# One fused attention and gated MLP kernel, its 1134 operations put in another order

## The chip, the cores and the metric

The kernel runs on one core of a Trainium2 chip. Its engines work side by side, each on its own instructions in the order given: TensorE (PE in the profile, with its weight loads as PEld), VectorE (DVE), ScalarE (ACT), GpSimd (POOL), and SyncE (SP), whose queue issues the transfers. They hand over through semaphores. The metric is the device time of one execution in microseconds. Before the change the median of three runs is 200.47 us (199.44 to 200.6).

## The reference

Two stages. The first is causal attention on 4 batches of 8 heads, 768 positions, 64 channels, in which each query sees only the six chunks of 32 keys with the highest bound:

```python
k_min, k_max = min and max of each chunk of 32 keys
ub = sum_d maximum(q * k_min, q * k_max)          # one bound per query and chunk
ub = where(causal, ub, -1e9); top_chunks = the 6 largest per query
scores = q @ k.T / 8, kept where the chunk is in top_chunks and causal
attn = softmax(scores); x = attn @ v              # heads side by side: 4 x 768 x 512
```

The second is a gated MLP with a spatial product over the 768 positions:

```python
h = maximum(x @ w_in, 0); u, v = halves of h      # 512 columns each
v_n = (v - mean(v)) / sqrt(var(v) + 1e-6)
v_s = w_spatial @ v_n + b_spatial
out = (u * v_s) @ w_out
```

## The kernel before, in words

Two heads make a pair: pairs 0 to 15, four to a batch. The first four pairs are worked in halves of 384 positions, a and b. After each batch's four pairs comes its MLP, six tiles of 128 rows; MLP work of one batch stands between attention work of the next.

The code builds a list of named operations with their inputs, outputs and buffer pools (`load` L502, `prep` L523, `attend` L716, `mlp` L865). A string, `ORDER` (L160), then says in which order they are issued, on which engine and in which buffers. A word such as `c_k0aA:0` is operation c_k0a on ScalarE with place 0 of its pool; P is TensorE, D VectorE, A ScalarE, G GpSimd, S the SP queue. `replay` (L115) takes the words one by one and checks that inputs come first and buffers are free, and the operations are emitted in that order (L997 and on). No scheduler moves anything afterwards. Each engine keeps its own words in the string's order, so an operation that waits holds back all later words of its engine.

The operations of a pair, by name: ld_k, ld_q, ld_v load; c_k, c_q, c_v cast to fp16 (the helper `copy`, L310, whose lines are L312 on ScalarE and L314 on VectorE and GpSimd); t_ transposes on TensorE (L561) and e_ brings the result out of PSUM; from pair 10 on x_kq transposes by DMA instead (L569), c_s spreads the queries for the wide form and kw copies the keys for it. kmm are the chunk maxima and minima (L593, VectorE), km their copy into place, rq the relus of q (L607 to L611), ub the bound's product (L628), max its eight largest (L650, L655), grd a guard column (L665, L667), sel the selection mask (L678 to L683), tsel and es its transpose (L701), sc the scores (L745 and L758, L780 in the wide form), exp the exponentials (L794, ScalarE), tri the causal cut of the diagonal (L805, GpSimd), av the product with v (L828), rec and nrm the division (L834, L839), tx, ex and xx the transposes of x (L860, L849).

Of the MLP: v and u are the two projections (L877) with relus rv and ru (L884 ScalarE, L886 VectorE); bn, ag, ln, rs the statistics (L895 to L904), vn the normalisation (L909, VectorE); s the spatial product (L925), g the gate (L929), xg or tg and eg the transpose of the gated tile (L950, L938), o the last product (L961), eo its copy out of PSUM, so the store (L968). c_wv, c_wu, c_wo and ld_ws, c_ws, tws, ews prepare the weights. The operations w0 to w3 (L453) are products of zeros, nine, three, five and two of them, that keep TensorE going at the start. presets (L434 to L437, L986) clear buffers; preset_kw copies `expand` into the wide key buffers.

PSUM holds two pairs of banks for scores and four general buffers (`gen`); SBUF has eight places for raw loads (`st`), nine half-size ones (`hst`), seven for exponentials and so on:

```python
RINGS = {"hst": 9, "st": 8, "kqT": 6, "kq16": 2, "x16": 2, "x16d": 2, "e": 7, "vraw": 6, "fold": 1, "sn": 3, "selT": 5, "qs": 2}
WARM = (9, 3, 5, 2)
```

The relus of q may run on GpSimd in the halves of the first pairs; the old order puts none there:

```python
op(f"rq{m}_{tag}", {"DVE": 465.0 if half is None else 265.0, "ACT": t_act(ns) + 40.0,
                    **({} if half is None else {"POOL": 1450.0})}, go, ...)
```

The numbers beside the engines are costs for whoever searches an order; nothing in the program reads them when it is replayed.

Of the kernel before, what the change touches and what calls it, by code (L numbers as in the profile page):

```python
# [163 lines left out]
ub0aP:2 max0aD:0 c_k3aG:3 grd0aG:0 t_q1aP:3 c_k1aA:0 expandA:0 t_k1aP:0 sel0aD: c_k2aG:1 e_k1aA:1 c_k0bG:2 t_k3aP:1  # L164
tsel0aP:2 t_k2aP:0 es0aD:0 e_q1aA: rq1_1aA:1 kmm1_1aD:1 preset_km0G: kmm0_1aD: km0_1aG:3 km1_1aG: ld_q2aS:8 c_q2aG:0
e_k2aA:2 e_k3aA:3 c_q3aA:3 preset_sn1G: kmm0_2aD:2 kmm1_2aD: sc0a_0P:10 t_k0bP:3 ub1aP:2 t_q2aP:0 t_q3aP:1 ld_q1bS:0
ld_q0bS:1 kmm0_3aD:0 c_q1bG:1 c_q0bD:2 ld_k1bS:2 ld_k3bS:3 ld_wu1S:0 ld_k2bS:4 ld_q2bS:5 ld_q3bS:7 ld_k4S:1 ld_v1aS:6
max1aD:1 preset_vt5G: grd1aG:0 c_k1bG:0 preset_km4D: exp0a_01A:0 km0_2aG:0 exp0a_00A: e_q2aA: km1_2aA: e_k0bA:
c_k3bG:3 sel1aD: ld_v0aS:8 ld_ws1S:2 ld_q4S:3 ld_v3aS:0 ld_q7S:4 ld_wv0S:5 ld_v2aS:1 ld_wv3S:6 ld_k5S:7 e_q3aD:
rq1_2aD:0 rq1_3aD:1 kmm1_0bD:1 kmm0_0bD: w0P:0 tsel1aP:0 t_q1bP:2 t_q0bP:3 t_k3bP:1 es1aA:1 ub2aP:0 sc1a_0P:10  # L170
km1_0bG: e_q1bA: e_q0bA: preset_snb1D: max2aD:0 kmm1_3aD: sel2aD:0 c_k2bG:1 c_q2bG:2 km0_0bA: rq1_0bA:0 grd2aA:
km0_3aG:4 km1_3aG: ub0bP:2 tsel2aP:3 max0bD:1 es2aD:2 sel0bD:1 e_k3bA: exp1a_00A:1 exp1a_01A: c_q3bG:3 ub3aP:0
t_q2bP:1 t_k1bP:3 e_k1bA: e_q2bA: c_wu1G:0 rq1_1bD:0 max3aD:0 sel3aD:0 preset_vt2D: c_v0aA:1 c_k4G:2 c_v1aG:3
preset_snb0D: t_k2bP:2 sc2a_0P:10 exp2a_00A:2 exp2a_01A: e_k2bD: grd3aG: grd0bG: av1aP:3 tsel3aP:1 tsel0bP:0
kmm1_1bD:2 es3aD:3 kmm1_2bD:1 rec1aD:0 kmm1_3bD:0 kmm0_1bD: av0aP:2 t_k4P:1 rec0aD:1 kmm0_3bD: nrm1aD:0 nrm0aD:1
kmm0_2bD: rq1_2bA:1 es0bA:4 c_q4G:0 e_k4A:4 km0_1bG: c_ws1G:1 c_v3aG:5 km1_1bG: sc3a_0P:10 exp3a_00A:3 exp3a_01A:
t_q3bP:0 t_q4P:1 e_q4A: e_q3bD: tws1P:3 ub1bP:2 max1bD:0 ews1D:0 sel1bD:0 c_q7G:2 sc0b_0P:10 c_v2aG:2 c_wv0G:0 tx0aP:0
av2aP:1 km0_2bA: km1_2bG: av3aP:3 ex0aD:0 rec2aD:2 nrm2aD:1 grd1bA: tsel1bP:2 ub2bP:0 max2bD:1 rec3aD:0 exp0b_01A:4
exp0b_00A: tx2aP:1 sc0b_1P:01 nrm3aD:1 tx3aP:3 c_k5G:3 c_wv3G: preset_sna1G: tri0b_00G: km1_3bG: ld_wu2S:0 c_wu2G:
km0_3bG: grd2bA:1 es1bA:0 rq1_3bA:0 ld_wv1S:1 ld_wv2S:3 ld_q6S:2 ld_wu3S:4 ld_k6S:5 c_wv2G: c_wv1G: sel2bD:  # L180
exp0b_11A:5 exp0b_10A: ex2aD: ex3aD: kmm1_4D:2 t_q7P:2 rq1_4D:1 e_q7D:5 kmm0_4D: t_k5P:0 km0_4G:2 tx1aP:1 ex1aA:
e_k5A:0 tsel2bP:3 sc1b_0P:10 ub3bP:1 max3bD:0 sel3bD:0 v0_1P:0 rv0_1D:0 c_k6D:0 es2bD:1 km1_4G: grd3bG: c_wu3G:
tri0b_10G: exp1b_01A:6 exp1b_00A: v0_2P:2 sc1b_1P:01 tsel3bP:1 rv0_2A:1 ld_v0bS:2 ld_wu0S:7 c_wu0D: c_q6D:1 es3bD:2
c_v0bG: ld_v1bS:3 ld_q5S:6 ld_k8S:0 ld_q9S:3 exp1b_10A:1 exp1b_11A: t_k6P:0 av0bP:2 e_k6A:1 bn0_1D:0 bn0_2D:1
tri1b_10G: c_q5G:2 tri1b_00G: c_q9G:3 ld_ws2S:1 c_ws2G:0 ld_ws5S:4 ld_k7S:5 ld_v4S:7 ld_v2bS:4 ld_ws0S:2 ld_v3bS:5
ld_k9S:6 t_q6P:3 ub4P:1 e_q6A: sc2b_0P:01 max4D:1 rec0bD:1 nrm0bD:1 ag0_1D:0 t_q5P:0 u0_1P:3 u0_2P:2 exp2b_01A:0
exp2b_00A: tri2b_00G: c_k8D:1 c_v1bD: rq1_6D:0 preset_km1D: sel4D:1 e_q5D: kmm0_5D:1 kmm1_5D: ru0_1A:0 ru0_2A:1 grd4A:
# [28 lines left out]
tri9_10G: grd11G: c_s12G:0 tri9_00G: rv1_2A:3 km0_12A: v1_4P:3 o0_5P:0 ag1_1D:2 rq0_12D: ub12P:2 bn1_2D:1 exp9_20A:2
exp9_21A: eo0_5A:2 eo0_4A:1 rv1_4D:4 bn1_5D:2 sc10_0P:10 exp10_01A:6 exp10_00A: v1_3P:0 av8_0P:3 av8_1P:1 sc10_1P:01
ld_q15S:7 xs11S:3 ld_k14S:4 so0_4S: ld_v11S:1 x_kq13S:4 max12D:0 ag1_5D:3 sel12D: ag1_2D: bn1_0D:0 rec8_0D:2 bn1_4D:2
rec8_1D:1 rv1_3A:0 ld_v10S:3 ld_v12S:5 ld_q14S:6 tri9_20G: av9_1P:2 u1_3P:0 nrm8_1D:0 bn1_3D:1 ag1_0D: exp10_11A:1
# [813 lines left out]
```

## Time and profile before

| | us |
|---|---|
| median of three runs | 200.47 |
| the profiled execution | 198.78 |
| its span, first to last instruction | 197.1 |
| TensorE busy | 186.9 |
| VectorE busy | 163.0 |
| ScalarE busy | 144.5 |
| GpSimd busy | 89.9 |
| granted TensorE clock | 1.000 |

The durations below come from the profiled execution, whose own time is 1.7 us under the median. Groups of the profile read: line, engine, operation, output<-input, shapes, count | busy us, mean ns of one | idle time of the engine before them and what ended it. Stretches of time are given from the start of the span. Matmuls overlap their neighbours, so that a busy TensorE may have small holes, and a matmul's mean duration is longer than the distance to the next one.

### The profile page before, as it was taken

The page shows a single profiled execution, that of the slowest core. Times are in us where ns is not written, and L with a number is a line of the kernel's source. Part 1 is how long each engine was busy: PE and PEld are TensorE (multiplying, and loading weights), DVE is VectorE, ACT ScalarE, POOL GpSimd, SP SyncE. Part 2 cuts the span into 40 slices and gives each one's busy share as a digit, 9 for nine tenths or more (in the row PEclk, how much of TensorE's full clock was granted, in tenths as well). Part 3 has the DMA queues.
Part 4 walks back from the last instruction along what each step waited for, and adds up shares of the span by engine and source line. Part 5 has one row for each costly group of instructions (what it writes and reads, how often), then busy time and mean ns, then how long its engine had stood idle before and what let it go on. Part 6 is the DMA issues. An engine that isn't in the chain of part 4 may idle for free.

```text
span 197.1 us, 5797 instructions
## 1 busy us (share of the span) xinstructions
PE 186.9 (95%) x2201; PEld 107.7 (55%) x2201; DVE 163.0 (83%) x499; ACT 144.5 (73%) x233; POOL 89.9 (46%) x175
## 2 busy tenths in 40 slices
PE   7799989999999899999999999999999999999992
PEld 2356665566656255664367566545675664444450
DVE  2798999999899999997999999996995644894521
ACT  3889999889999976896898895598877541464051
POOL 3479696758578886553343191245540410000000
PEclk9999999999999999999999999999999999999999
DMA  5999999999998969699999999895930357501654
GB/s 161 315 325 350 331 321 330 336 255 327 235 251 199 245 137 168 145 188 192 286 221 283 243 172 149 189 241 174 253 69 0 92 121 216 161 37 71 161 213 160
DMA packets 98139, 41.01 MB, mean 208 GB/s; under 512 B 85440, under 2 KB 92864, under 8 KB 98112
## 3 DMA queue, kind: packets, MB, share of 16 engines
q1 hardware_dynamic: 97968, 40.38, 81.9%
q8 instruction: 17, 0.28, 0.6%
q10 hardware_dynamic: 144, 0.26, 0.3%
q14 instruction: 10, 0.08, 0.1%
HBM read 24.38 MB, written 6.29 MB: 156 GB/s over the span
## 4 chain that ended last, share of the span: by engine, by line
PE 70%; DVE 20%; issue 3%; DMA 2%; POOL 1%; ACT 1%; SPq 1%; DVEq 0%; POOLq 0%
PE gen L877 16%; PE gen L925 15%; PE gen L961 10%; PE gen L828 8%; PE sc L780 6%; DVE kmm L593 6%; PE sc L745 4%; PE sc L758 3%; DMA early<-in_k_dram 2%; PE gen L561 2%; PE gen L628 2%; DVE x L839 2%; DVE max L655 2%; DVE vn L909 2%; DVE stats L895 1%
## 5 line engine op out<-in xcount | busy, mean ns | idle before, releaser
L794 ACT ACTIVATE e<-sc 128x768 f16<-128x768 f32 (+1 forms) x96 | 83.0, 918 | 18.4 <-PE sc L780 10.2
L805 POOL TENSOR_SCALAR_AFFINE_SELECT e<-e 128x512 f16<-128x512 f16 (+1 forms) x44 | 27.8, 636 | 38.0 <-ACT e L794 33.1
L925 PE MATMUL gen<-vn,wsT 128*128 128x512 f16 x144 | 34.4, 379 | 0.9 <-DVE wsT L314 0.9
L593 DVE TENSOR_REDUCE kmm<-kqT 128x24 f16<-128x768 f16 (+1 forms) x40 | 30.4, 779 | 0.1
L929 DVE SCALAR_TENSOR_TENSOR late<-gen,bcol,u 128x512 f16<-128x512 f32 x24 | 17.7, 745 | 14.4 <-PE gen L925 11.9
L828 PEld LDWEIGHTS <-e 128*128 128x128 f16 x672 | 23.4, 97 | 4.1 <-issue 0.8
L828 PE MATMUL gen<-vt,e 128*128 128x65 f16 x672 | 24.7, 192 | 0.3 <-DVE u L886 0.3
L961 PE MATMUL gen<-w_out,late 128*128 128x512 f16 (+1 forms) x100 | 23.4, 371 | 0.0
L312 ACT ACTIVATE late<-gen 128x512 f32<-128x512 f32 (+1 forms) x20 | 11.5, 598 | 15.6 <-PE gen L961 15.6
L925 PEld LDWEIGHTS <-wsT 128*128 128x128 f16 x144 | 13.5, 98 | 16.4 <-issue 2.3
L745 PE MATMUL sc<-kqT 64*128 64x128 f16 (+2 forms) x212 | 17.0, 271 | 0.3 <-ACT e L794 0.3
L780 PE MATMUL sc<-kqT,early 128*128 128x256 f16 (+2 forms) x132 | 16.7, 268 | 0.0
L895 DVE BATCH_NORM_STATS2 stats<-vraw 128x6 f32<-128x512 f32 x24 | 15.9, 676 | 0.5 <-ACT vraw L884 0.4
L655 DVE MAX8 max<-gen 128x8 f32<-128x20 f32 (+4 forms) x160 | 14.8, 165 | 0.3 <-ACT kqT L312 0.3
L961 PEld LDWEIGHTS <-late 128*128 128x128 f16 x100 | 9.4, 98 | 9.7 <-issue 0.7
L877 PEld LDWEIGHTS <-early 128*128 128x128 f16 x96 | 8.8, 97 | 10.5 <-issue 0.9
L884 ACT ACTIVATE vraw<-gen 128x512 f32<-128x512 f32 x16 | 9.4, 603 | 6.0 <-PE gen L877 5.6
L877 PEld LDWEIGHTS <-xT 128*128 128x128 f16 x96 | 8.8, 97 | 8.4 <-issue 0.5
L780 PEld LDWEIGHTS <-early 128*128 128x128 f16 x132 | 10.8, 98 | 4.7 <-DMA kqT<-qs 0.3
L909 DVE TENSOR_SCALAR vn<-vraw,mv,rstd 128x512 f16<-128x512 f32 x24 | 12.7, 579 | 0.4 <-ACT rstd L904 0.4
L312 ACT ACTIVATE kqT<-gen 128x384 f16<-128x384 f16 (+1 forms) x20 | 11.9, 623 | 1.3 <-PE gen L561 1.3
L314 POOL CAST n<-st 128x768 f16<-128x768 f32 x14 | 11.8, 848 | 0.5 <-DMA st<-in_q_dram 0.2
(115 smaller groups left out, 334.9 us busy)
## 6 DMA issues: line engine op xcount, KB each, us to landing
out_dram<-late SPq DMA_DIRECT2D x22, 256.0 KB, 2.7
st<-in_k_dram SPq DMA_DIRECT2D x12, 384.0 KB, 4.7
st<-in_q_dram SPq DMA_DIRECT2D x12, 384.0 KB, 5.3
st<-in_v_dram SPq DMA_DIRECT2D x12, 384.0 KB, 4.5
st<-in_moe_w_spatial_dram SPq DMA_DIRECT2D x6, 384.0 KB, 5.4
st<-in_moe_w_in_dram SPq DMA_DIRECT2D x8, 256.0 KB, 4.9
early<-in_k_dram SPq DMA_DIRECT2D x8, 192.0 KB, 4.4
early<-in_q_dram SPq DMA_DIRECT2D x8, 192.0 KB, 4.5
```

Of the source, the lines that this page charges most:

```text
L312: e.activation(out=out, in_=in_, func=Act.Copy)
L593: lambda e, m=m, f=f, x=x, w=w: e.tensor_reduce(kmm.t[:, m, 0:nch], x().rearrange("d (c j) -> d c j", j=w), axis=AX.X, op=f, negate=(m == 1)),
L655: e.max(m8.t[:, t - tiles[0], s, :], ub.t[:, a:a + CPT * (t + 1)])
L745: e.matmul(sc[z].t[:, a:a + len(qs) * P].rearrange("p (t c) -> p t c", c=P), lhsT=kq.t[r, 0, t * P:(t + 1) * P], rhs=qv[r, qs[0]:qs[-1] + ...
L780: e.matmul(sc[z].t[:, a:a + len(qs) * P].rearrange("p (t c) -> p t c", c=P), lhsT=st["kw"].t[:, hi, t // 2, t % 2 * P:(t % 2 + 1) * P], rh ...
L794: e.activation(out=e_.t[:, z, :, 0:w], in_=x.t.rearrange("p (h c) -> p h c", h=2)[:, :, 0:w], func=Act.Exp, scale=scale)
L805: e.affine_select(out=d, in_=d, compare_op=Alu.is_ge, fill=0.0, base=0, channel_multiplier=-1, pattern=[[0, 2 * len(zs)], [1, P]])
L828: e.matmul(avv()[:, n, hi, :], lhsT=es[g].t[:, zz, hi, c:c + P], rhs=vt.t[:, t, hi, 0:D + 1], start=(t == 0), stop=(t == qi))
L877: e.matmul(acc.t, lhsT=x.t[:, ko, t * P:(t + 1) * P], rhs=w.t[:, ko, :], start=(ko == 0), stop=(ko == NDO - 1))
L895: op(f"bn{b}_{t}", {"DVE": t_dve(DH)}, lambda e, t=t, stats=stats: e.bn_stats(stats.t, vraw[t].t), reads=[vraw[t]], writes=[stats])
L925: e.matmul(acc.t, lhsT=wsT.t[:, s, t * P:(t + 1) * P], rhs=vn[s].t, start=(s == 0), stop=(s == NQT - 1))
L961: e.matmul(acc.t[:, 0:w], lhsT=gT.t[:, a2 * KO + ko, :], rhs=w_out.t[:, ko, c0:c0 + w], start=(ko == 0), stop=(ko == KO - 1))
```

## The change

Only `ORDER` changes. The 1134 words name the same operations. 152 of those on compute engines stand on another engine: 41 from ScalarE to VectorE and 38 the other way, 17 from ScalarE to GpSimd and 24 back, 19 from VectorE to GpSimd and 13 back. One relu of q (rq1_1b) goes from VectorE to GpSimd; three stores change between the SP queue and ScalarE's. Buffer places change with the order. Nearly every line of the string differs; these are its beginning, the stretch around the first batch's normalisation and spatial products, the place of the relu, the one of pair 14's v, and the end:

```diff
 ORDER = """
-ld_k0aS:0 ld_q0aS:1 ld_q1aS:2 ld_k1aS:3 ld_k3aS:4 ld_k2aS:5 ld_q3aS:6 ld_k0bS:7 zeroD:0 epsG:0 preset_vt1D: identG:0
-ones24D:0 preset_km2D: ex24D:0 c_k0aA:0 preset_sna0G: firstD:0 w2P:0 w1P:1 t_k0aP:0 c_q0aG:1 t_q0aP:1 w3P:0
-preset_km3D: e_k0aD:0 kmm0_0aD:0 kmm1_0aD: preset_vt3D: e_q0aA: c_q1aA:2 km1_0aA:2 triG:0 km0_0aG: lowG:0 rq1_0aD:0
+ld_k0aS:0 ld_q0aS:1 ld_q1aS:2 ld_k1aS:3 ld_k3aS:4 ld_k2aS:5 identG:0 preset_sna0G: preset_snb0G: preset_km2G:
+preset_km4G: zeroD:0 preset_vt2D: cmaskG:0 triG:0 c_q0aG:0 lowG:0 firstD:0 c_k0aD:1 w3P:0 w1P:1 ones24D:0 t_k0aP:0
+e_k0aA:0 kmm0_0aD:0 kmm1_0aD: t_q0aP:1 e_q0aA: preset_vt0D: rq1_0aD:0 km0_0aG:2 preset_vt3D: ex24D:0 km1_0aA: c_k1aA:2
+c_q1aD:3 c_k2aG:1 ld_q2aS:6 ld_q0bS:7 ld_k0bS:8 w2P:0 expandA:0 ub0aP:2 max0aD:0 c_q2aG:0 preset_km3D: sel0aD:0
...
+ld_wv1S:5 ld_k5S:6 ld_wv2S:7 ld_wu1S:0 nrm0aD:1 grd0bA: km1_1bA: km0_1bA: e_k4A:4 rq1_1bG:0 c_wv3G:0 c_v2aG:3
...
-rs0_1A: exp5_21A:3 exp5_20A: vn0_4D:2 vn0_3D:3 vn0_5D:4 vn0_1D:5 c_wo2D: ub7P:3 tws4P:2 u0_5P:1 kmm0_8D: ews4D:
-max7D:0 sel7D:1 ru0_5A:5 sc6_0P:10 s0_0P:1 s0_1P:2 c_v9A:3 exp6_00A:4 exp6_01A: km0_8A:2 rq1_8A:0 ld_wo0S:0 c_wo0G:
+km0_7G: preset_qs1G: tri5_00G: tri4_20G: c_v5G:4 tws4P:0 ews3D: e_k9D: ag0_4D: ews4D: ag0_3D: sc5_1P:10 exp5_10A:2
+exp5_11A: ub7P:2 tws5P:1 u0_5P:3 ln0_1A:1 ru0_5A:5 rs0_1A: sc5_2P:10 exp5_21A:3 exp5_20A: max7D:1 grd7G:1 sel7D:
+ews5D: t_q8P:0 tsel7P:2 av4_1P:3 av4_0P:1 tri5_10G: c_q11G: tri5_20G: c_k10G:1 ld_q10S:5 bcolS:0 c_q10G: sc6_0P:01
+kmm1_8D:2 vn0_5D:1 vn0_0D:2 vn0_3D:3 rec4_0D:2 vn0_1D:4 vn0_4D:5 rec4_1D:0 nrm4_0D:0 kmm0_8D: es7A:1 av5_0P:2 e_q8A:
+exp6_00A:4 exp6_01A: s0_0P:0 sc6_1P:01 g0_0D:0 av5_1P:1 s0_1P:0 kmm1_9D:1 rec5_0D:1 nrm4_1D: kmm0_9D: g0_1D: rec5_1D:2
+ld_wo0S:7 c_wo0A: nrm5_1D: ld_v7S:3 x_kq11S:4 nrm5_0D: x_kq10S:5 ld_k12S:6 ld_wo3S:0 xg0_1S:0 exp6_11A:1 exp6_10A:
+km1_8A:2 rq1_8A:1 sc6_2P:10 s0_2P:3 exp6_20A:5 exp6_21A: preset_kw0G: preset_kw1G: c_v7A:2 c_v6D:0 tri6_00G: c_s10G:1
+km0_8G: ub8P:0 sc7_0P:10 exp7_00A:6 exp7_01A: rq1_10D:0 max8D:0 tri6_10G: tri6_20G: rq1_9D:1 km1_9A:4 s0_3P:1 av6_0P:2
...
+eo1_2A:0 o1_3P:3 av12_1P:1 rec12_1D:2 nrm12_1D: sc14_1P:10 xs15S:2 so0_3S: xg1_5S:0 so1_2S: ld_v14S:2 exp14_11A:0
...
+rs2_0A: vn2_3D:4 vn2_2D:5 ru2_5D:2 vn2_0D:0 vn2_1D:1 c_v14D:3 vn2_4D:2 c_v15G:1 tri14_00G: tri14_10G: sc14_2P:01
...
-so2_3S: u3_4P:1 s3_5P:0 o3_0P:2 ru3_4D:0 g3_5D:0 o3_1P:3 tg3_5P:1 eo3_0A:2 eo3_1A:0 eg3_5A:1 o3_3P:0 s3_4P:2 eo3_3A:1
-o3_2P:3 g3_4D: tg3_4P:1 o3_6P:0 eg3_4D: o3_5P:2 so3_1S: so3_0S: so3_3S: eo3_2A:0 so3_2A: eo3_6D:2 eo3_5D: so3_6S:
-so3_5S: o3_4P:3 eo3_4A:1 so3_4S:
+s3_3P:1 s3_2P:2 u3_5P:0 s3_4P:3 g3_3D:0 g3_2D: so2_3S: so2_5S: xg3_1S:0 xg3_3S:1 o3_0P:1 g3_4D:1 eo3_0D:0 o3_1P:2
+tg3_4P:3 s3_5P:1 eg3_4A:0 eo3_1D:2 o3_2P:2 so3_1S: so3_0S: eo3_2A:1 so3_2S: o3_3P:3 eo3_3A:2 so3_3S: o3_4P:2 eo3_4A:0
+so3_4A: ru3_5D:4 g3_5D: tg3_5P:0 eg3_5D: o3_6P:1 o3_5P:3 eo3_6D:1 eo3_5A: so3_5A: so3_6S:
 """
```

At the start the first cast of k goes from ScalarE to VectorE and the copy of its transpose the other way, and two and three dummy products stand ahead of the first transposes with five behind, where five and three stood ahead and two behind. At the end the last row tile's product, split into two halves of 256 columns (o3_6 and o3_5), comes last, where it stood before the whole product of the tile before it (o3_4).

More of the change, by code (lines that the diff above doesn't have):

```diff
@@ L166 @@
[L166 to L175, printed above, removed]
@@ L216 @@
[L216 to L219, printed above, removed]
-nrm8_0D: ag1_3D: rec9_1D:0 ag1_4D: exp10_10A: ln1_0A:2 rs1_0A: u1_1P:1 sc10_2P:10 ru1_3A:6 ln1_1A:3 rs1_1A:
```

142 lines of the change are left out of this document (73 added, 69 removed).

## The prediction

> **What bounds the kernel now.** I read the engines' totals, then the busy time by stage, then the chain of work that ended last, then the groups by shape. The totals:
>
> ```profile
> PE 186.9 (95%) x2201; PEld 107.7 (55%) x2201; DVE 163.0 (83%) x499; ACT 144.5 (73%) x233; POOL 89.9 (46%) x175
> ```
>
> TensorE (PE) is nearly full, and its work is the same in both orders, so an order can only win back TensorE's gaps. Where they lie, by stage (start:end, length, then busy time and instructions of PE, PEld, DVE, ACT, POOL):
>
> ```profile
> 0.00:16.00 16.00, 12.76 (x136) 7.13 (x137) 10.58 (x45) 11.63 (x26) 8.85 (x33) 1.00 0.91 271
> 16.00:28.00 12.00, 10.88 (x199) 7.75 (x197) 11.63 (x52) 11.35 (x22) 9.96 (x22) 1.00 1.03 345
> 28.00:65.20 37.20, 36.73 (x594) 22.59 (x591) 36.07 (x108) 35.23 (x55) 26.56 (x46) 1.00 1.02 276
> 65.20:67.80 2.60, 1.66 (x13) 0.60 (x8) 2.60 (x6) 2.60 (x5) 2.48 (x4) 1.00 1.17 212
> 67.80:86.00 18.20, 18.20 (x275) 10.23 (x275) 17.64 (x61) 14.38 (x22) 13.42 (x24) 1.00 0.81 168
> 86.00:160.00 74.00, 73.47 (x809) 43.48 (x806) 64.06 (x191) 58.05 (x86) 28.63 (x51) 1.00 0.87 183
> 160.00:193.10 33.10, 33.05 (x201) 15.93 (x197) 20.46 (x41) 10.68 (x22) 0.00 (x0) 1.00 0.44 136
> 193.10:197.10 4.00, 0.19 (x1) 0.00 (x0) 0.00 (x0) 0.60 (x1) 0.00 (x0) 1.00 0.44 163
> ```
>
> Up to 67.8 us VectorE (DVE) is saturated and TensorE, though it looks busy, has holes; from there to 193.1 TensorE lacks 0.53 + 0.05 us in 107; then come 4.0 us of tail. The chain says what held the first spatial products (line 925) back (start, length, what):
>
> ```profile
> 62.98 0.45 issue
> 63.42 2.22 DVE vn L909 x4
> 65.64 0.77 DVE w_out L314
> 66.42 0.86 DVE kmm L593
> 67.28 0.47 DVE wsT L314
> 67.79 1.46 PE gen L925 x6
> ```
>
> So there are three places to win: VectorE's path to 67.8, the 0.58 us after it, and the tail.
>
> **VectorE's waits behind GpSimd.** The same kind of VectorE instruction takes very different times:
>
> ```profile
> L314 DVE CAST kq<-st 128x768 f16<-128x768 f32 x3 | 4.3, 1423 | 0.0
> L314 DVE CAST n<-st 128x768 f16<-128x768 f32 x3 | 2.1, 688 | 0.0
> L314 DVE CAST vt<-st 128x768 f16<-128x768 f32 x2 | 1.1, 548 | 0.0
> L314 DVE CAST w_out<-st 128x512 f16<-128x512 f32 x1 | 0.8, 850 | 0.0
> L909 DVE TENSOR_SCALAR vn<-vraw,mv,rstd 128x512 f16<-128x512 f32 x24 | 12.7, 579 | 0.4 <-ACT rstd L904 0.4
> ```
>
> and in order of time (start, length, what):
>
> ```profile
> 114.27 2.78 DVE L314 CAST kq<-st 128x768 f16<-128x768 f32 x1
> 114.27 1.59 POOL L314 CAST vt<-st 128x768 f16<-128x768 f32 x2
> 115.81 0.82 POOL L314 COPY early<-kqT 64x768 f16<-64x768 f16 x1
> ```
>
> A cast of 768 columns takes 548 ns free and 2.78 us when it meets three GpSimd instructions in a row. The waits sum to 3 x (1423-548) + 3 x (688-548) + about 300 (850 against at most 548) for the casts, some 3.3 us, and the vn group has more. But the long one lies at 114 us, where TensorE doesn't wait. On the path to 67.8 lie only: two n casts, 0.4; the w_out cast, 0.3; the issue gap, 0.45; and 2.22 - 4 x 0.46 (0.46 is the spacing of free ones) = 0.4. Together **1.55 us**.
>
> [...]
>
> **The change, term by term.** VectorE's pure work. Relus of v and u change hands 13 to 13: nothing. Output copies: 7 come, 2 and a half-width one go, so +4.4 of these:
>
> ```profile
> L314 DVE COPY late<-gen 128x512 f32<-128x512 f32 x4 | 2.7, 684 | 1.2 <-PE gen L961 1.1
> L611 DVE TENSOR_SCALAR rq<-kqT 128x768 f16<-128x768 f16 x8 | 4.3, 543 | 0.0
> ```
>
> that is +3.0 us. Relus of q: 4 whole ones fewer at 0.54, three halves go and one comes (at half of that): -2.7. Casts: seven whole ones go, three come, two of 512 columns go, one half goes and four come, one copy more of the wide queries: about 4 x 0.55 + 0.9 - 4 x 0.35 (half of the 688), or -1.7. Evacuations of transposes, wide-key copies and presets about cancel (+1.1, +0.5, -0.5, -0.3). Net some -0.6 us of 163, worth nothing by itself.
>
> What counts is where it stands. With the group means, counted op by op: ahead of the first spatial product the new order puts 1.9 us more free VectorE work and 0.7 us more TensorE work. The lead, free VectorE work required ahead of a TensorE operation minus TensorE work ahead of it, is at most 4.3 in the old order on the way to 68 us (second spatial product: 58.9 us against 54.6), 5.9 with the 1.55 of waits. In the new order it is 4.4 there, but climbs to 5.9 by 86 us (av7_0, the probabilities times the values of pair 7: 76.0 against 70.1) with no wait counted. So the middle gains nothing even if every wait vanishes, and loses each wait that stays. Against that the old order loses another 0.5 us between 67.8 and 86 in spaces that the busy time covers (18.2 us for 17.7 us of products, counted at the spacing of the stretch after 160 us). I put the two at **0**, with -0.8 (no waits) and +2 (as many as now) as ends.
>
> The head. The first cast and the turn of k swap engines, and five dummy products instead of three and two stand around:
>
> ```profile
> 1.25 3.20 PE L453 MATMUL sc<-w_out 128*128 128x512 f16 x8 [1.25 <-DVE vt L434]
> 4.96 0.59 PE L453 MATMUL sc<-w_out 128*128 128x512 f16 x2
> 6.63 0.19 PE L628 MATMUL gen<-km,kqT 128*128 128x24 f16 x1 [1.08 <-ACT km L312]
> ```
>
> VectorE casts 384 columns in some 0.35 us (half of the 688) where ScalarE took 0.5, and its idle places before 16 us (16.00 - 10.58 = 5.4) get casts to fill them. I take **-0.3**; ends 0 and -1.0.
>
> After 86 us the lead falls to 2 and then below zero, where the old order keeps 3 to 6. Of TensorE's 0.58 of gaps these two are VectorE's:
>
> ```profile
> 120.93 0.46 PE L828 MATMUL gen<-vt,e 128*128 128x65 f16 x10 [0.31 <-DVE u L886]
> 132.85 1.02 PE L877 MATMUL gen<-w_v,xT 128*128 128x512 f16 x4 [0.20 <-DVE u L886]
> ```
>
> They can go: **-0.5**; ends -0.58 and +1, since a wait that no old row shows (a slot, a late load) may come. One such is near: the load of v for pair 14 stands behind a store whose copy waits for a product 12 us of TensorE work ahead of the third batch's spatial products, and its cast stands ahead of one of their vn on VectorE; I count 0.3 to 1.5 us of margin.
>
> The tail. Now the last product is whole and its store 256 KB; the new order ends with the two half-width products:
>
> ```profile
> 191.15 0.40 PE L938 MATMUL gen<-ident,late 128*128 128x128 f16 x4
> 191.66 1.23 DVE L314 COPY late<-gen 128x512 f16<-128x512 f16 x3 [0.56 <-PE gen L938]
> 193.32 0.60 ACT L312 ACTIVATE late<-gen 128x512 f32<-128x512 f32 x1 [1.47 <-PE gen L961]
> ```
>
> and of the stores (KB each, us from issue to landing):
>
> ```profile
> out_dram<-late SPq DMA_DIRECT2D x22, 256.0 KB, 2.7
> out_dram<-late SPq DMA_DIRECT2D x2, 128.0 KB, 1.8
> ```
>
> They need the transposes' evacuation at once, with nothing between: 0.51 us to its start and about 0.42 for it, less some 0.2 in which the transposes issue, plus 0.1 of hand-over: +0.8 of idle TensorE. Back come 0.2 on the copy and 0.9 on the smaller store, of which, with two stores at once, I take 0.6. Net **0**; ends -0.3 and +0.6.
>
> One relu of q (384 columns) goes to GpSimd, a form that the trace lacks. The nearest rows:
>
> ```profile
> L805 POOL TENSOR_SCALAR_AFFINE_SELECT e<-e 128x512 f16<-128x512 f16 x40 | 26.1, 659 | 37.9 <-ACT e L794 33.1 <-issue 4.7
> L314 POOL CAST n<-early 128x384 f16<-128x384 f32 x11 | 5.7, 523 | 3.9 <-DMA early<-in_q_dram 2.5 <-DMA early<-in_k_dram 0.7 <-PE gen L561 0.5
> ```
>
> The cast of that width, 523 ns, and the select of 512 columns, 659, are the bounds; I take 0.6. It hides in GpSimd's idle time (12.00 - 9.96 from 16 to 28 us); without that cover it is late by its length. 0.
>
> Sum: 0 - 0.3 - 0.5 + 0 = -0.8 us. The profiled execution took 198.8 us (span 197.1); that gives 198.0. The median of the runs is 200.5, 1.7 above it, so **199.7**.
>
> **Rivals.** (a) *All waits go and the head fills up.* -0.8 - 1.0 - 0.6 - 0.3 = -2.7, so 197.8. For it: VectorE's waits are real. Against: five vn still stand in a row while GpSimd has casts due.
>
> (b) *The waits only move.* +2 in the middle in place of 0: 200.5 - 0.8 + 2, or 201.7.
>
> (c) *GpSimd becomes the bound, and the kernel slower.* Between the km copies of head pair 7 and those of pair 8 the new order places one 128x1536 memset, five selects, four casts, four copies of expand, one copy of wide queries, one guard and a km copy:
>
> ```profile
> L314 POOL CAST vt<-st 128x768 f16<-128x768 f32 x8 | 6.6, 825 | 0.0
> L314 POOL COPY early<-expand 64x768 f16<-64x768 f16 x4 | 3.4, 842 | 0.2
> L986 POOL MEMSET qs<- 128x1536 f16 x1 | 1.4, 1378 | 0.0
> ```
>
> 1.4 + 5 x 0.66 + 5 x 0.83 + 4 x 0.84 + 0.5 = 12.7 us, in a stretch where TensorE has 11.9 us of work; the old order requires none of it there. The selects wait for exponentials (33.1 us in the row), and casts queue behind them. [...] With three waits of 1 us handed on to VectorE's maxima and back, +3: 202.7. For it: from 60 to 82 us 19.8 us of GpSimd's work are required, and its selects wait. Against: it may run ahead, since its first inputs are early.
>
> [...]
>
> **How the numbers follow.** Forecast 0.43, (a) 0.22, (b) 0.13, (c) 0.18, (d) 0.04. One per cent, 2 us, is about what a measurement of this kernel tells from no change. Faster by that is below 198.5: nearly all of (a) and a little of the forecast, 0.25. Slower, above 202.5: most of (c) and the upper part of (b), 0.22; within, 0.53. The range cuts a part of (a) and of (c): 196.8 to 203.2. The forecast's own is 198.7 to 200.9.
>
> **What would show it.** Right: in the chain the first spatial products wait for vn directly; TensorE's idle after 86 us is below 0.5 beside the one gap of 0.9 before the last two products; DVE busy is some 159 to 162. Casts of 768 columns near 550 ns on VectorE show (a); vn means above 620 show (b). [...] Wrong altogether would be a wait for DMA in the first 30 us that holds GpSimd's casts.

## The result, and the profile after

The new order takes 197.42 us (median of six runs, 196.46 to 198.43) against 200.50 before (199.44 to 200.60): ratio 0.987, with a 95% interval of 0.983 to 0.991 (the two medians alone give 0.985). That is 3.1 us by the medians, within the range, 2.3 us under the forecast of 199.7 and below the forecast's own 198.7 to 200.9. The profiled execution of the new order took 197.71 us, its span 196.0, where the old one took 198.78 and 197.1. So the two profiles differ by only 1.1 us. The other 2.0 us are in no trace: the old order's profiled execution is 1.7 us below the median of its runs, the new one's is 0.3 above. What the two profiles can explain is the 1.1.

The engines' totals after:

```profile
PE 185.7 (95%) x2201; PEld 107.6 (55%) x2201; DVE 162.1 (83%) x496; ACT 143.9 (73%) x237; POOL 93.8 (48%) x174
```

The busy time by stage, cut as in the prediction but for the stretch from 86 to 160 us, which is parted at 112, and the end (start:end, length, then busy time and instructions of PE, PEld, DVE, ACT, POOL, the granted clock, the DMA share and GB/s):

```profile
0.00:16.00 16.00, 13.46 (x144) 7.53 (x145) 12.65 (x52) 12.18 (x27) 9.31 (x34) 1.00 0.92 269
16.00:28.00 12.00, 11.04 (x186) 7.26 (x186) 11.73 (x50) 9.78 (x18) 8.96 (x19) 1.00 1.01 314
28.00:65.20 37.20, 36.67 (x620) 23.60 (x618) 36.09 (x117) 35.85 (x56) 30.56 (x56) 1.00 1.07 280
65.20:67.80 2.60, 2.60 (x46) 1.43 (x45) 2.60 (x6) 1.97 (x3) 2.49 (x3) 1.00 0.67 149
67.80:86.00 18.20, 17.89 (x268) 9.90 (x267) 18.12 (x61) 16.83 (x26) 11.69 (x20) 1.00 1.03 205
86.00:112.00 26.00, 23.65 (x260) 12.69 (x259) 20.46 (x68) 21.03 (x35) 14.62 (x21) 1.00 1.09 214
112.00:160.00 48.00, 48.00 (x517) 29.93 (x516) 41.55 (x113) 34.51 (x53) 16.17 (x25) 1.00 0.76 152
160.00:192.70 32.70, 32.18 (x177) 15.25 (x172) 18.63 (x37) 11.35 (x23) 0.00 (x0) 1.00 0.49 153
192.70:196.00 3.30, 0.17 (x2) 0.00 (x0) 0.25 (x1) 0.38 (x1) 0.00 (x0) 1.00 0.42 151
```

And the stretch from 86 to 160 us of the old order, parted at the same place:

```profile
86.00:112.00 26.00, 25.98 (x320) 14.46 (x317) 24.34 (x85) 21.45 (x34) 7.96 (x14) 1.00 1.14 235
112.00:160.00 48.00, 47.49 (x491) 29.02 (x490) 39.72 (x107) 36.60 (x53) 20.68 (x37) 1.00 0.73 154
```

Three things are to be seen. VectorE has 2.1 us less idle time in the first 16 us (12.65 busy against 10.58). This is at the good end: in the nine profiles of kernels that begin as the new order VectorE is idle for 3.4 to 5.1 us there, in the two of the old order for 5.4 and 5.9. The hole of 0.94 us ahead of the second spatial product is gone. And a new hole has come between 86 and 112 us, where TensorE idles 2.35 us instead of 0.02.

Busy time hides small holes (from 67.8 to 86 us before, 18.2 us of it held 17.7 us of products by their spacing), so I also worked out TensorE's lag: for each of its operations (one word of the order) the distance to the start of the next, less the distance that the quickest fifth of its kind shows in the two traces, summed up to a time. It says how much TensorE has lost by then (us):

| up to | before | after | best2 (below) |
|---|---|---|---|
| 30 us | 7.2 | 6.5 | 5.6 |
| 64 us | 9.2 | 8.0 | 7.3 |
| 88 us | 11.5 | 9.4 | 8.7 |
| 112 us | 12.3 | 12.6 | 11.0 |
| 185 us | 13.7 | 12.7 | 11.0 |

The new order is 0.7 us ahead at 30 us and 2.1 at 88. Between 88 and 112 it gives back 2.4 of them, wins 1.3 later where the old order still loses, and the end is even: 0.7 us of idle TensorE ahead of the last two products against 0.7 less behind the last (the span ends 3.1 us after it instead of 3.8). That is the 1.1.

What TensorE waited for at 112 us, in order of time (start, length, engine, line, operation; in brackets the idle time ahead and what ended it; all lines of the new kernel are one less than before):

```profile
107.98 0.82 POOL L313 COPY early<-kqT 64x768 f16<-64x768 f16 x1
...
108.19 1.52 DVE L908 TENSOR_SCALAR vn<-vraw,mv,rstd 128x512 f16<-128x512 f32 x1 [0.24 <-ACT rstd L903]
...
108.76 0.63 POOL L804 TENSOR_SCALAR_AFFINE_SELECT e<-e 128x512 f16<-128x512 f16 x1
109.34 1.04 POOL L313 CAST kq<-st 128x768 f16<-128x768 f32 x1
...
109.73 1.98 DVE L908 TENSOR_SCALAR vn<-vraw,mv,rstd 128x512 f16<-128x512 f32 x2
...
111.77 1.47 PE L924 MATMUL gen<-vn,wsT 128*128 128x512 f16 x6 [1.58 <-DVE vn L908]
```

Three normalisations (vn) of batch 1 took 1.52, 1.02 and 1.04 us, where free ones take 0.54, each beside GpSimd's work. The first began at 108.19 us, beside a copy, and ended at 109.71, beyond a select that began at 108.76 and took 0.63. The groups say the same of the whole:

```profile
L908 DVE TENSOR_SCALAR vn<-vraw,mv,rstd 128x512 f16<-128x512 f32 x24 | 15.3, 666 | 2.7 <-ACT rstd L903 2.7
L313 DVE CAST vt<-st 128x768 f16<-128x768 f32 x3 | 1.8, 585 | 0.0
L610 POOL TENSOR_SCALAR rq<-kqT 128x384 f16<-128x384 f16 x1 | 1.5, 1505 | 0.0
```

The vn cost 2.6 us more than before (579 ns each), while VectorE's casts of 768 columns are down to 585 and, for the one kq cast left, 543 ns. The waits beside GpSimd's work have not gone, they have moved from the casts to the vn. The relu of q on GpSimd took 1.505 us.

### The profile page after: what moved, and what is told of

It is laid out like the page before. It is cut to its first block, busy times and chain, and to the rows that moved or that the text cites. A ratio compares the mean times of both kernels' runs of the same rounds, so it can differ in the third digit from the quotient of the medians.

```text
span 196.0 us, 5795 instructions
## 1 busy us (share of the span) xinstructions
PE 185.7 (95%) x2201; PEld 107.6 (55%) x2201; DVE 162.1 (83%) x496; ACT 143.9 (73%) x237; POOL 93.8 (48%) x174
## 4 chain that ended last, share of the span: by engine, by line
PE 70%; DVE 8%; DMA 6%; POOL 4%; ACT 3%; SPq 3%; issue 3%; POOLq 0%; DVEq 0%; ACTq 0%
PE gen L876 18%; PE gen L924 14%; PE gen L960 10%; PE gen L827 8%; PE sc L779 6%; PE sc L744 5%; PE sc L757 3%; DMA st<-in_k_dram 2%; PE gen L627 2%; SPq L513 2%; POOL n L313 2%; DMA early<-in_q_dram 2%; PE gen L560 2%; DMA st<-in_moe_w_in_dram 2%; ACT e L793 2%
## 5 line engine op out<-in xcount | busy, mean ns | idle before, releaser
L311 ACT ACTIVATE late<-gen 128x512 f32<-128x512 f32 (+2 forms) x16 | 9.4, 586 | 19.6 <-PE gen L960 9.5
L908 DVE TENSOR_SCALAR vn<-vraw,mv,rstd 128x512 f16<-128x512 f32 x24 | 15.3, 666 | 2.7 <-ACT rstd L903 2.7
L313 POOL CAST n<-st 128x768 f16<-128x768 f32 x17 | 13.8, 823 | 3.5 <-PE gen L560 1.8
L876 PEld LDWEIGHTS <-early 128*128 128x128 f16 x96 | 9.1, 97 | 10.5 <-issue 0.8
L779 PEld LDWEIGHTS <-early 128*128 128x128 f16 x132 | 11.0, 98 | 5.2 <-issue 0.4
L311 ACT ACTIVATE kqT<-gen 128x384 f16<-128x384 f16 (+1 forms) x18 | 10.9, 627 | 2.8 <-PE gen L560 2.8
L876 PE MATMUL gen<-w_v,xT 128*128 128x512 f16 x48 | 11.8, 379 | 0.0
```

The lines of the kernel that those rows point to most:

```text
L311: e.activation(out=out, in_=in_, func=Act.Copy)
L313: e.tensor_copy(out, in_)
L779: e.matmul(sc[z].t[:, a:a + len(qs) * P].rearrange("p (t c) -> p t c", c=P), lhsT=st["kw"].t[:, hi, t // 2, t % 2 * P:(t % 2 + 1) * P], rh ...
L876: e.matmul(acc.t, lhsT=x.t[:, ko, t * P:(t + 1) * P], rhs=w.t[:, ko, :], start=(ko == 0), stop=(ko == NDO - 1))
```

## The experiments

Each kernel was timed beside the kernel before, and the ratio is to that. The intervals are some 0.4% to either side, about 0.8 us, so differences between these kernels of less than a microsecond are read from the profiles, not from the medians. A profile is of one execution, though, and where the same instructions scatter as much as a change does, this is said.

**The kernel before, once more.** Nothing is changed.

> The kernel before, unchanged, profiled once more. Its first profile (198.8, 1.7 under its median) has TensorE's products of zeros at 0.42 us apart until 3.9 us and at 0.21 after; the other profiles of this study change between 5 and 10 us, and those that change late took longer. If that change at the start is what makes executions differ, an execution near 200.5 shows it later than 4.5 us and TensorE up to 1.7 us later by 30 us than in the first profile. If not, the first 30 us are as in the first profile and the time is lost behind them. The ratio is 1.000 but for noise.

Ratio 0.9985 (0.9959 to 1.0012); median 200.44. The new profile is of an execution of 198.66 us, again the fastest of its kernel and 1.8 us below the median, though its start was slow:

```profile
1.25 3.60 PE L453 MATMUL sc<-w_out 128*128 128x512 f16 x8 [1.25 <-DVE vt L434]
4.64 0.85 PE L561 MATMUL gen<-ident,n 128*128 128x128 f16 x6
5.28 1.06 PE L453 MATMUL sc<-w_out 128*128 128x512 f16 x2
```

All ten products of zeros are 0.42 us apart; in the first profile the last two took 0.59 together instead of 1.06. TensorE's lag at 30 us is 7.9 instead of 7.2, but by 130 us both stand at 13.0: it is made up on the way. So the start doesn't explain why the old order's timed executions are 1.8 us above its profiled ones. (The old body behind the new head, below, was profiled at its fastest too. Of the nine kernels that begin as the new order three were, and their profiles lie on both sides of their medians.)

A part of the gap goes with the granted clock. Beside these experiments the old order was timed in 62 executions. In 38 of them the mean granted clock was 0.987 to 0.991, and their median is 200.7 us; in 14 it was 1.000, as in both profiles, and their median is 199.7. The new order's six read 0.997 to 1.000. One stretch of 3.4 us at half clock, as the kernel with one product of zeros shows below, makes a mean of 0.991 over 197 us. So about 0.8 us of the 1.8 goes with the clock. That the clock is the cause is not shown, and where in the old order it falls is in no trace. The rest, from 199.7 to the profile's 198.7, stays open.

**Head and body apart.** The first 106 words of the new order (to some 14 us) ahead of the old rest, and the first 94 words of the old order ahead of the new rest:

```diff
 h_newhead:  <words 1 to 106 of the new order> <all other operations as in the old order>
 h_oldhead:  <words 1 to 94 of the old order>  <all other operations as in the new order>
```

> The first 106 words of the new order (to about 14 us), then every other operation in the old order with the old engines. Head theory: in the profiles VectorE is idle for 5.3 us of the first 16 in the old order and 3.0 in the new one, and it bounds everything up to the first spatial products, so this alone gives about 2 us: 198.5 against 200.5, VectorE's idle time before 64 us near 4.5 instead of 6.6, the second spatial product some 2 us earlier than 67.8. Body theory (the gain came from what stands behind the head): 200.2, and the idle time comes back later as waits.

> The first 94 words of the old order, then every other operation in the new one. Head theory: the new order loses what it had gained by 64 us, about 2 us: 199.4 against its own 197.4, VectorE's idle time before 64 us near 6.5. Body theory: 197.7.

Both are slower than either kernel: 202.05 us (ratio 1.011, 1.008 to 1.015) and 202.65 us (1.012, 1.008 to 1.016). Neither theory has it. The first two stages of the new head with the old body:

```profile
0.00:16.00 16.00, 12.50 (x122) 6.42 (x122) 11.88 (x48) 10.51 (x24) 8.73 (x35) 1.00 0.85 244
16.00:28.00 12.00, 9.78 (x191) 7.28 (x185) 10.05 (x43) 10.29 (x18) 8.34 (x18) 1.00 0.99 318
```

VectorE does 1.3 us more by 16 us than in the old order (11.88 against 10.58) and 1.6 less in the next 12 (10.05 against 11.63). The idle time is not filled by the head alone; it is put off.

The old head with the new body was profiled at its slowest, 204.74 us. There GpSimd's cast waits 4.4 us for a load, TensorE 3.1 us for the cast behind it (waits of 13 to 30 us), and then the granted clock is at half for 6.8 us (stretches as above, the clock in the third column from the right):

```profile
POOL w_v L311 <- DMA st<-in_moe_w_in_dram: 4.4, 1, 4.4
...
PE gen L825 <- POOL vt L311: 3.1, 1, 3.1
```

```profile
23.57:26.98 3.41, 1.58 (x28) 1.09 (x27) 2.51 (x11) 3.37 (x8) 0.00 (x0) 1.00 0.92 257
26.98:33.81 6.83, 5.52 (x71) 4.28 (x70) 3.53 (x15) 2.37 (x4) 6.49 (x14) 0.50 0.99 336
```

All six of its executions have a mean granted clock of 0.970 to 0.992. Each mixture is an order of its own, with waits that neither whole order has, so these two don't tell which part of the new order wins the time.

**More work for VectorE.** One chunk minimum at 17 us is done three times, and in another kernel one at 95.7 us twice:

```diff
         for o in plan.done:
             o.fn(E[o.eng])
+            for _ in range(2 if o.name == "kmm1_2b" else 0):    # the other kernel: 1, "kmm1_12"
+                o.fn(E[o.eng])
```

> The new order with one chunk minimum of VectorE (384 columns, at 17 us) done three times, so 0.92 us more of VectorE's work there and nothing else. If VectorE bounds the new order from there to 82 us, TensorE is 0.9 later at 76 and 88 us, and after that the time depends on the stall at 109: 0.6 to 0.9 more at the end, 198.2. If GpSimd's casts or the loads bound the first 30 us (the chain of the new order runs through GpSimd from 21 to 30 us), less than 0.3: 197.5.

> The new order with one chunk minimum of 768 columns at 95.7 us done twice: 0.86 us more of VectorE's work. TensorE lost 3.2 us between 88 and 112 us in the new order. If VectorE's amount of work sets that, 0.8 more: 198.2. If the waits for ScalarE and GpSimd set it (VectorE is idle 4.6 of those 24 us), less than 0.3 more: 197.5.

At 17 us: TensorE loses 4.0 us between 16 and 30 us instead of 3.0. The loss comes at once: from the scores of pair 2 to those of pair 3 it is 1.9 us, and 0.8 in each of the nine other profiles with these products. So VectorE's 0.92 us pass to TensorE in full there; VectorE bounds that part. That the loss lasts is not shown: at 64 us the lag is 9.7 against 8.0, of which 0.8 were there at 16 us, but from the scores of pair 2 to those of pair 6, at 63 to 66 us, this kernel loses 5.1 us and the nine others 3.9 to 5.6. The median, 198.09 (0.987, 0.983 to 0.991), is 0.7 higher, which its interval can't tell from nothing. At 95.7 us: TensorE loses 2.8 us between 88 and 112 us, where the new order lost 3.2 and four other kernels with its words there 2.4 to 3.5; the median is 197.18 (0.981, 0.977 to 0.985). There the added work costs nothing that can be seen; the waits do.

**The casts beside the normalisations.** In casts1 four operations of GpSimd go behind a cut of the diagonal, which was meant to wait for exponentials:

```diff
-tri10_10G: kw1_12G c_q15G ... kw0_12G ... tri10_00G: c_k15G: ... exp10_20A: rs1_0A: ... c_v10G:4 ... tri10_20G:
+tri10_10G: kw1_12G c_q15G ... exp10_20A: tri10_20G: tri10_00G: c_v10G:4 kw0_12G: c_k15G: rs1_0A: ...
```

and in casts0 two casts and what hangs on them go behind the first cut of pair 6 (the transpose of pair 10 on the SP queue also goes behind two loads, not shown):

```diff
-c_k10G:1 ld_q10S:5 bcolS:0 c_q10G: ... exp6_00A exp6_01A: ... preset_kw0G: preset_kw1G: ... tri6_00G: c_s10G km0_8G
+ld_q10S:5 bcolS:0 ... exp6_00A exp6_01A: tri6_00G: c_k10G:1 c_q10G: c_s10G km0_8G preset_kw0G: preset_kw1G: ...
```

> The new order with four GpSimd operations (one cut of the diagonal, the casts of v10 and k15, a copy of wide keys) moved behind the cut that waits for the next exponentials, so that they don't run beside the normalisation of batch 1. GpSimd theory: vn of batch 1 takes 1.52, 1.02 and 1.04 us where a free one takes 0.54, TensorE waits 1.7 us for them at 109 to 112 us; with the casts gone they take 0.55 each, the wait falls below 0.5, and the time falls by 1.2 to 1.7 us, to about 196. Statistics theory (ScalarE's and VectorE's chain of statistics, relus and exponentials sets that wait): the vn get short, TensorE waits at least 1.2 us all the same, and the time is within 0.4 of the new order's 197.4.

> The new order with the casts of k10 and q10 and the copies of expand on GpSimd moved behind the first cut of pair 6, out of the normalisation of batch 0. There two vn take 0.75 and 1.04 us where a free one takes 0.54. If VectorE bounds all up to 82 us, the 0.7 us saved reach the end: 196.7. If another engine is as late there (GpSimd, ScalarE), the vn get short and less than 0.2 comes of it: 197.3; a loss of up to 1 us would say that the moved casts are late for the transposes that wait for them.

casts1: 197.22 us (0.985, 0.982 to 0.988). The three vn fall to 0.85, 0.75 and 0.53 us, and what TensorE loses ahead of the spatial products falls from 1.7 to 0.3; its lag at 112 us is 11.6 instead of 12.6. That is the GpSimd theory's sign. But by 150 us the lag is 12.6, as without the change. What took it back (waits of 125 to 133 us: engine, line, releaser, us in all, times, longest; and the queue's transposes):

```profile
DVE kmm L591 <- DMA kqT<-kq: 1.2, 1, 1.2
...
PE gen L875 <- DVE u L884: 0.4, 1, 0.4
```

```profile
116.91 1.65 SPq L948 DMA_TRANSPOSE late<-late  x1
118.67 1.76 SPq L567 DMA_TRANSPOSE kqT<-kq  x1
```

The keys of pair 14 are transposed by the SP queue no earlier than in the new order (issued at 118.67 us, there at 118.57), and the transpose lands at 124.22 us, there at 121.95. That is 2.3 us later than in the new order, and not as late as there, as the expectation of best1 below has it. The chunk minima wait for it, and VectorE is late behind them.

casts0: 197.09 us (0.984, 0.981 to 0.988). The last vn of batch 0 falls from 1.04 to 0.53, and the cast of v6 seven microseconds later rises from 0.66 to 1.20. A wait was taken from one instruction and given to another. From 30 to 88 us TensorE loses 3.0 us as against 2.9. By the lag the second outcome, less than 0.2, is what came; the median's 0.3 us is within the interval.

**The next limit, and the one behind it.** best1 has both moves, and the transpose of pair 14 goes ahead of a load, a store and a gate's transpose; best2 moves that gate's transpose up as well:

```diff
 best1:
-x_kq15S:3 ld_v12S:4 so0_5S: ... xg1_1S:1 x_kq14S:0 xx9S:0
+x_kq15S:3 x_kq14S:0 ld_v12S:4 so0_5S: ... xg1_1S:1 xx9S:0
 best2:
+x_kq15S:3 x_kq14S:0 xg1_1S:1 ld_v12S:4 so0_5S: ... xx9S:0
```

> The moves of casts0 and casts1 together, and the transposing load of pair 14's queries and keys issued ahead of a store and a gate's transpose instead of behind them: with casts1 alone the 1.2 us won at 109 us were lost again at 128 to 131 us, where chunk minima waited until 124.2 us for that transpose, as late as in the new order without the moves. If that queue order is the cause, the 1.2 us stay: 196.0. If VectorE is the bound there, 197.0.

> As best1, but the transpose of the first gated tile of batch 1 goes ahead of a load and a store on the SP queue. In best1 it stood behind them, began at 117.5 us, and TensorE waited 1.6 us for it at 121. If these transposes, one after the other on one queue, are what takes the gains of casts1 back, TensorE's lag keeps below that of the new order by 1.2 us or more to the end: 196.2. If it comes back in another place, 197.2, and it is named.

best1 took 198.44 us (0.989, 0.984 to 0.994). The 1.2 us came back as a single wait at 121 us, 1.6 us by the lag, for the gate's transpose, which landed at 123.16 us (the waits of 118 to 124 us, where the weight load's is longer, and the queue):

```profile
PEld L959 <- DMA late<-late: 1.9, 1, 1.9
```

```profile
117.46 1.75 SPq L948 DMA_TRANSPOSE late<-late  x1
```

best2 took 196.87 us (0.981, 0.978 to 0.985), and TensorE loses nothing from 112 us on (11.0 at 112 us and at 185). It is clearly faster than the kernel before. That it is faster than the new order (0.987, 0.983 to 0.991) is not shown, since the intervals overlap. In the profiles a lead of 0.9 us was there at 30 us, ahead of all the moved words, and 0.7 at 88. From 88 us on it loses 2.3 us, the new order 3.3, and four other kernels with the new order's words there about 2.4 to 3.5. Its vn of batch 1 still wait, 0.86, 0.75 and 1.04 us, since the cut that was to hold GpSimd back did not wait at all:

```profile
107.39 1.40 POOL L803 TENSOR_SCALAR_AFFINE_SELECT e<-e 128x512 f16<-128x512 f16 x2
107.45 0.86 DVE L907 TENSOR_SCALAR vn<-vraw,mv,rstd 128x512 f16<-128x512 f32 x1 [0.25 <-ACT rstd L902]
...
108.33 1.71 DVE L907 TENSOR_SCALAR vn<-vraw,mv,rstd 128x512 f16<-128x512 f32 x2
```

**The rest of the waits, and the end.** best3 puts a cut that does wait ahead of GpSimd's work, and at the end the last tile's transposes ahead of the whole product o3_4:

```diff
-tri10_10G: kw1_12G:1 c_q15G:1 ... tri10_20G: tri10_00G: c_v10G:4 kw0_12G: c_k15G: ... tri11_00G:
+tri10_10G: c_q15G:1 c_k15G: ... tri11_00G: tri10_20G: tri10_00G: c_v10G:4 kw1_12G:1 kw0_12G:
-o3_4P:2 eo3_4A:0 so3_4A: ru3_5D:4 g3_5D: tg3_5P:0 eg3_5D: o3_6P:1 o3_5P:3
+ru3_5D:4 g3_5D: tg3_5P:0 eg3_5D: o3_4P:2 eo3_4A:0 so3_4A: o3_6P:1 o3_5P:3
```

> best2 with two more moves. On GpSimd, the first cut of pair 11, which waits for exponentials, now stands ahead of two cuts, the cast of v10 and two copies of wide keys, and the cast of k15 goes ahead of batch 1's normalisation: in best2 three vn still took 0.86, 0.75 and 1.04 us beside such work, and TensorE waited 0.8 for them. At the end, the transposes of the last gated tile go ahead of the whole product o3_4 instead of behind it (its gate is done 1.7 us before they run in the new order). If these waits are what is left, the vn take 0.55, the wait of 0.7 before the last two products is gone, and the time is 1.2 to 1.4 less than best2: 195.6. If the end is set by the stores, the last product ends earlier and nothing comes of it: 196.8 less at most 0.8 for the vn.

196.92 us (0.981, 0.978 to 0.985): no different from best2. Yet both waits went:

```profile
109.65 0.55 DVE L907 TENSOR_SCALAR vn<-vraw,mv,rstd 128x512 f16<-128x512 f32 x1
110.22 0.96 DVE L907 TENSOR_SCALAR vn<-vraw,mv,rstd 128x512 f16<-128x512 f32 x2
111.50 1.46 PE L923 MATMUL gen<-vn,wsT 128*128 128x512 f16 x6
```

and in the chain of the end (start, length, what) the transposes, o3_4 and the halves follow without a hole, where now ScalarE's copies and their store's issue come one after the other:

```profile
190.43 0.22 PE gen L936 x4
190.65 0.88 PE gen L959 x4
191.53 0.02 issue
191.55 0.61 ACT late L310
192.16 0.02 issue
192.18 0.38 ACTq L966
```

From the last product's end to the end of the span it is 3.5 us instead of 3.1, so 0.3 of the 0.7 went to the copies; and 0.5 were lost at 122 us. Its profile fell on a late start (7.9 us of lag at 30 us, where best2's had 5.6), which makes up for the rest. From 30 us on it loses 5.0 us, best2 6.0 with its 0.7 at the end. That shows in no median.

**The relu back on VectorE.**

```diff
-rq1_1bG:0
+rq1_1bD:0
```

> The new order with the one relu of q (rq1_1b) back on VectorE, where it takes 0.34 us in place of 1.51 on GpSimd. GpSimd theory: GpSimd stands in the chain from 21 to 30 us, so its casts come 1.5 us earlier, and 0.2 to 0.6 is won against the 0.34 that VectorE pays: 197.1. VectorE theory: 0.3 lost, 197.7.

197.54 us (0.985, 0.981 to 0.990), as the new order. GpSimd's 1.5 us bought nothing that shows. Its next cast then waits for its load (idle time in brackets), and the first cast of 768 columns behind that starts at 22.03 us, where it starts at 22.00 in the new order (this execution's first bound came 0.7 us later than that one's):

```profile
20.59 0.61 POOL L312 CAST w_v<-st 128x512 f16<-128x512 f32 x1 [0.83 <-DMA st<-in_moe_w_in_dram]
```

**One product of zeros instead of five.**

```diff
-WARM = (9, 3, 5, 2)
+WARM = (9, 3, 1, 2)
```

> The new order with one product of zeros in place of five between the first two transposes and the first bound's products. Queue theory: at the slow rate the five take 2.1 us and hold back the first bound's products (at 6.3 to 7.5 us in the profiles) that VectorE waits for; with one they start at 6.2 always, and what is lost up to there reaches the end: 0.4 to 0.9 less, 196.7, and less scatter between executions. Warm-up theory: with fewer products TensorE's rate doubles later, the transposes and first scores take twice as long for it, and it is 0.3 to 1 more: 198.1.

198.25 us (0.988, 0.983 to 0.992): no gain. Both theories have half of it. The first bound's products start at 6.28 us, as in the new order's profile, but then TensorE falls back towards half its rate. Six products of the first scores, here and then in the new order:

```profile
8.95 0.82 PE L744 MATMUL sc<-kqT 64*128 64x128 f16 x6
```

```profile
8.46 0.50 PE L744 MATMUL sc<-kqT 64*128 64x128 f16 x6
```

TensorE had lost 4.1 us by 16 us instead of 3.5. The granted clock shows the fall:

```profile
4.94:8.36 3.42, 1.65 (x23) 0.94 (x22) 2.90 (x16) 2.82 (x7) 0.84 (x3) 1.00 0.98 306
8.36:11.77 3.41, 3.41 (x40) 2.26 (x40) 2.74 (x7) 2.58 (x7) 1.63 (x5) 0.50 1.09 346
```

The five products, which are in no result, are worth about what they cost.

## Why the prediction was right or wrong

**From the profile to the median: the step that failed.** The sum gave 198.0 us for the profiled execution; it took 197.7. Then 1.7 was added because the old order's median lies that far above its profile, and the new order's doesn't. Of the 2.3 us of error, 2.0 are this step. The second profile of the old order shows that its gap is no accident (1.8 again). About 0.8 of it goes with the granted clock, 0.987 to 0.991 in most of its executions and 1.000 in both profiles, and the new order's executions read 0.997 to 1.000; the rest is open. With another execution of the new order in the profile the 2.0 would be another number: profiles of the kernels that begin as it does lie from 1.2 us below their medians to 1.7 above.

**The sum was near by errors that cancel.** By the lag, in us:

| step | forecast | measured |
|---|---|---|
| head (to 30 us) | -0.3 | -0.7 |
| middle (30 to 88 us) | 0 | -1.4 |
| after that, without the tail | -0.5 | +1.1 |
| tail | 0 | 0.0 |

These are two executions. In the eight other profiles with the new start TensorE loses 3.0 to 4.3 us in the middle, where the new order's lost 2.9 and the old order's 4.3: the -1.4 is at the good end.

*Head and middle.* The lead that I counted was right as a lead: 5.9 us at av7_0, and TensorE was there at 81.9 us, 11.8 behind the 70.1 of its own work (counted as in the prediction, which takes shorter durations than the table of the lag). But the lag there is the lead, plus the waits, plus VectorE's idle time at the start, and I took that last term to shrink by 0.3. It shrank by 2.1 (12.65 against 10.58 busy in 16 us; by 64 us it is 4.7 idle against 6.9). I had named the 5.4 us of idle places and then priced the head by one cast. The first probe shows that work put in at 17 us is paid in full at once, not that it is still missing at 64 us; that the filling by itself is the cause was not shown, since the head alone did not carry it.

*Waits.* "The middle loses each wait that stays" held: vn of 666 ns, above the 620 that I gave as the sign of rival (b). On the way to 86 us they were a fifth, a half and a tenth of a microsecond (0.75 and 1.04 in batch 0, 0.66 for the cast of v6); the 2 us of them lay at 108 to 111 us.

*After 86 us.* The two small gaps of the old order are gone (48.00 of 48.00 us busy from 112 to 160), as forecast, and the load for pair 14 came in time. But TensorE's idle time from 86 us on, which was to stay below 0.5 us beside the gap at the end, is 2.35 us by 112 us alone. I gave +1 as the far end for "a wait that no old row shows". It came, at another place: I had the lead fall to 2 us by then and so left the vn of batch 1 out, though the first rival's own objection, several vn in a row while GpSimd has casts due, holds for them as well. A lead counts work, and the chain there runs through statistics on VectorE, two small steps on ScalarE between exponentials (rstd, 0.30 and 0.22 us), and back: in the second probe 0.86 us more of VectorE's work cost nothing that could be seen there.

*Tail.* 0.8 us of idle TensorE forecast, 0.7 measured by the lag and 0.52 in brackets here; 0.8 back forecast, 0.7 measured. Right in each term:

```profile
190.91 0.39 PE L937 MATMUL gen<-ident,late 128*128 128x128 f16 x4
191.34 0.42 DVE L313 COPY late<-gen 128x512 f16<-128x512 f16 x1 [2.09 <-PE gen L937]
191.82 1.05 PE L960 MATMUL gen<-w_out,late 128*128 128x256 f16 x8 [0.52 <-DVE late L313]
```

*The relu on GpSimd.* 0.6 us taken, 0.52 and 0.66 as bounds; it took 1.505. The cast and the select of like width did not bound it. With rq1_1b back on VectorE the same relu took 0.345 us, less than a quarter of GpSimd's 1.505. That it is hidden was right.

**Rivals.** (a) gives 197.8, close to the measured time, and its sign came (casts of 543 and 585 ns), but not its reason: the waits moved to the vn. (b) has its sign and not its time. Of the forecast's own signs none came cleanly: in the chain the first spatial products follow products of TensorE and not a vn, the idle time after 86 us is too long, and VectorE's 162.1 us are at the edge of 159 to 162. (c) did not come: GpSimd is in no piece of the chain between 60 and 82 us, and no product waited for a km there (one weight load stood 0.56 us behind a km copy, at 75.7 us). The three waits of 1 us in its sum were my estimate, and no run shows them; GpSimd's two casts of 768 columns beside the vn at 109 to 111 us took 1.04 and 1.10 us, where one at 24.09 us took 0.82. (d), at 0.04, stood for products still 0.4 us apart after 5 us. In the new order's profile the second five were 0.43 us apart until 5.5 us and 0.21 after, and took 1.55 us; in that of the kernel with the relu on VectorE they took 2.34. The granted clock of 1.00 in the rows of the first 16 us can't show this: the traces' record of the clock begins only at 3.9 us in the old order's first profile and at 5.4 in the new order's, what lies before it counts as 1.00, and products are 0.42 us apart there.

## What to carry to other kernels

Where one engine seems to bound a long stretch from its start, look at that engine's idle time ahead of and within the stretch when you price a new order, not only at the length of the operations that moved. A profile's own time and the median of plain runs can differ by more than the change, and the difference need not carry over: forecast against the profile, widen the range by it, and compare the granted clock of the profiled execution with that of the plain ones. And follow a gain to the last instruction: here 1.2 us won at 109 us were lost to a queue of transposes at 128, then to another of them at 121, before the third order's profile showed no loss behind 112 us.

## What the runs showed of the hardware

**The start of TensorE differs between executions of the same instructions.** The five products of zeros behind the first transposes, in the new order and in the kernel with the relu on VectorE, whose first 19 us hold the same instructions:

```profile
4.79 1.55 PE L452 MATMUL sc<-w_out 128*128 128x512 f16 x5
```

```profile
4.83 2.34 PE L451 MATMUL sc<-w_out 128*128 128x512 f16 x5
```

In the first the distance changes from 0.43 to 0.21 us at 5.5 us, in the second not within the five. The first bound's products then start at 6.28 or 6.96 us, and everything on VectorE up to 19 us moves with them. Nine profiles of kernels with this start have those products between 6.17 and 7.46 us; the two earliest are of executions of 196.0 and 196.2 us, the five latest of 197.6 to 199.3. The traces' clock records begin at 5.2 to 10.4 us in these nine: the five that begin before 6.5 us are of executions of 196.0 to 197.7 us, the four after 7 us of 197.6 to 199.3. The kernels are not the same, so this is a likely source of the scatter and not a proven one.

The granted clock changes within the traces. Its record begins, at 1.00, at 3.9 us in one profile of the kernel before and at 10.7 in the other, with the same instructions. In the kernel with one product of zeros it fell to 0.50 at 8.4 us, for 3.41 us; TensorE was busy for 1.65 of the 3.42 us ahead of that. In the old head with the new body it fell to 0.50 at 27.0 us, for 6.83 us; TensorE was busy for 1.58 of the 3.41 us ahead. In the old order's first profile TensorE was busy for 1.63 of the 3.42 us from 191.66 to 195.08 us, and the clock stayed at 1.00 to the end of the span. What makes it fall is not shown.

**VectorE instructions took longer beside several GpSimd instructions in a row**: 1.52 us for a vn that began beside a copy and ended behind a select, where free ones take 0.54, and 2.78 for a cast in the old trace, where a free one takes 0.55. Which instruction is hit differs between executions: in batch 0 the last three vn took 0.54, 0.75 and 1.04 us in the new order and, in casts1, where nothing ahead of them differs, 0.97, 0.93 and 1.04, and the first vn of the batch 0.53 and 1.10.
